# Attention feeding a max-out MLP on one core: the PE order and the evacuations laid out anew, the loads kept

## The chip, the core and the metric

The kernel runs on one core of one Trainium2 chip. The core has a matrix engine (TensorE, "PE" in the profile, with its weight loads as "PEld"), a vector engine (VectorE, DVE), an activation engine (ScalarE, ACT), a general engine (GpSimd, POOL), and a queue engine that issues transfers (SyncE, SP). Each engine works through its own instructions in their order and waits on semaphores for the others. The metric is the time of one execution on the device in microseconds (us); the median of several runs is given, with the lowest and the highest.

## The reference

Inputs are q, k and v of shape 8 x 8 x 1152 x 64 (batch, heads, sequence, width) and three weight matrices, all float32. Neighbouring rows of q are averaged, attention is computed with the 576 pooled queries against 1152 keys, and the result, 4608 tokens of 512 features, goes through a small MLP that takes the larger of two products.

```python
q_pool = q.reshape(B, H, S // 2, 2, D).mean(axis=3)
scores = np.matmul(q_pool, k.transpose(0, 1, 3, 2)) / np.sqrt(D)
attn = softmax(scores)                       # over the keys
x = np.matmul(attn, v)                       # -> (B * S/2, H * D)
out = np.maximum(x @ w1, x @ w2) @ w_out
```

## The kernel before, in words

Two heads are handled together as a pair; there are 32 pairs (4 for each batch entry). The MLP is rewritten: max(x w1, x w2) w_out = relu(x (w1 − w2)) w_out + x (w2 w_out). So there is one hidden product with `wd` = w1 − w2, and the output product adds a term with `w21` = w2 w_out.

The work consists of these kinds:

- **Loads** of q, k, v and weights, issued by SP (lines 343 to 383). Each waits until its raw buffer is free.
- **Casts** on POOL: keys (L405), pooled queries (L435), values (L445), and copies of the last 64 query columns of a pair's exponentials (L468, the "rest").
- **Transposes**: keys by a transfer on SP (`ktrans`, L475); queries by eight 32-row block transposes a pair on VectorE (`qtrans_dve`, L485), from pair 5 on. The first pairs use PE instead.
- **Score groups** (`scores`, L302): 324 groups of 512 columns for two heads. Each is made of 64-row matmuls that run in couples, one for each half of the array, and fills two PSUM banks. A pair has 10 and a bit of them.
- **Exponentials** (`exps`, L317) on ScalarE, one for each group, from the two banks to SBUF.
- **Value products** (`av_jobs`): a "chunk" is nine 128-row matmuls into one bank (L621); a pair has eight. A leftover of 64 query rows is 18 narrower matmuls (L636). VectorE divides by the row sums (L651, L654) and so empties the bank. Two jobs a pair; the last pair of each batch entry also takes the leftovers of the entry's four pairs.
- **Transposes of x** by transfers on SP or by PE, to `xT`.
- **Hidden products** (`h_jobs`, L760): eight couples of 64-row matmuls into two banks, up to 512 columns wide; then relu, on VectorE (L771) or ScalarE (L775).
- **Output products** (`p_job`, L803): 24 couples for 256 tokens into two banks, copied out by VectorE (L809) or ScalarE (L812), stored by SP. The last two blocks are made by `z_job` (L846).

In hidden and output jobs the second half of the couples uses the other row halves. Its first unit has a "fence": it waits on PE's own semaphore until the job's earlier matmuls have completed.

All banks come from eight PSUM banks. A job or a score group may write its banks only after the evacuation of what was there before.

**What sets the order.** Nothing is planned when the program is built: the order is written out as a string of 2712 letters near the end of the kernel (L959 to L987), one letter for one operation: `S` a score group, `E` an exponential, `A` one unit of a value job, `a` one evacuation of it, digits `0` to `3` a unit of an open MLP job (up to four open at once), `4` to `7` its evacuation on VectorE, `8`, `9`, `+`, `-` the same on ScalarE, `r` a query transpose on VectorE, `k`, `q`, `v`, `e` casts on POOL, `l` a load, `t` and `x` transposing transfers, `o` a store. `BANKS` names the bank that each score group or job takes, `MOE` the order of hidden and output jobs, `LOADS` the order of the loads. The function `step` (L925) turns each letter into an operation; the class `Plan` (L17) finds the semaphore waits from what each operation reads and writes. An engine's order is the order of its letters in the string; the place of a letter among those of other engines means nothing beyond the data it needs, with one exception. A load of q, k or v also waits for an exponential ("pace"), and which one depends on where the load stands in the string:

```python
def pace():
    g = done[0] - PACE          # done[0]: the last exponential in the string so far
    return [f"E{g}"] if PACE and g >= PACE_FROM else []
```

Of the kernel before, what the change touches and what calls it, by code (L numbers as in the profile page):

```python
# [116 lines left out]
def bass_funnel_attn__then__act_maxout2_kernel(  # L117
# [11 lines left out]
    E = moe_w_out.shape[1]  # L129
# [33 lines left out]
    FILLS = 16  # L163
    PACE = 2
    PACE_FROM = 40
    FOUR = 1
# [15 lines left out]
    )  # L182
    MOE = (
        "wwhhhhpphhhhpphhhhhhhhpphhhhpphhhhphhhhpphhhhphhhhphhhhpphhhhhhhhhphphh"
    )
    BANKS = (
        "0124605424023623462032424660232342630240624702402064202420472042646264246024604640164604264126402406"
        "0240260240246304260346204040640606062061262062062402740264062402406402640642704260202402402406401640"
        "6460462056204620462046042164206204620620426026402602602602604604614646046046024604604204620420642040"
        "6406406742064264264206520640260462620620162062046206240620206204230642042042424126426046046045620642"  # L190
        "6024062046206206206206412640246056046206404024024026423236042642042626260262626426454526420642064206"
        "2454"
    )

    ctx = ExitStack()
    with ctx:
# [131 lines left out]

        def pace():
            g = done[0] - PACE  # L330
            return [f"E{g}"] if PACE and g >= PACE_FROM else []

        done = [0]
        issued = [0]
# [8 lines left out]
        def load_k(i, lo=0, hi=NT, eng="SP"):  # L343
            b, h0, s = i // NHP, 2 * (i % NHP), i % 3
            old, name = behind() if eng == "SP" else ([], [])
            op(eng, lambda e: e.dma_start(  # L346
                kraw[s][:, :, lo:hi, :].rearrange("p h t d -> p h (t d)"),
                k[b, h0:h0 + 2, :, :].rearrange("h (p t) d -> p h (t d)", t=NT)[
                    :, :, lo * D:hi * D]),
                after=([f"kraw0.{c}" for c in K0] if s == 0 and hi - lo == NT else []) + pace() + old,  # L350
                w=([f"kraw0.{lo}"] if hi - lo < NT else [f"kraw{s}"]) + name,
                dma=f"d_kp{lo}" if hi - lo < NT else f"d_k{s}",
                cost=0.2 * (hi - lo) + 0.03 if hi - lo < NT else 1.45 + 0.6 * (i == 1), tag=("L", "k", i))

        def load_q(i, lo=0, hi=QU, eng="SP"):
# [6 lines left out]
                w=([f"qraw0.{lo}"] if hi - lo < QU else [f"qraw{s}"]) + name,  # L362
                after=(["qraw0.0", "qraw0.4"] if s == 0 and hi - lo == QU else []) + pace() + old,
                dma=f"d_qp{lo}" if hi - lo < QU else f"d_q{s}",
# [10 lines left out]
        def w_load(part, c):  # L375
# [5 lines left out]
                src.rearrange("(c p) f -> p c f", p=P)[:, c * n:(c + 1) * n, :]),  # L381
                w=[f"{key}{c}"] + name, after=old, dma=f"d_w{part}{c}", cost=1.34, tag=("L", "w", part, c))

# [541 lines left out]
        def step(c):  # L925
# [5 lines left out]
            elif c == "E":  # L931
                g, go = exp_at.pop(0)
                go()
                done[0] = g
            elif c in lines or c in "0123":
# [23 lines left out]
        for c in (  # L959
            "luFFlulllfyKQklgfbSkKEFlgFKSgESyFFlKEFgQSbESlFkSFEFFKlEySFSgESlqFFEFQlSbEFkSQElbKvSEgSlESceAAEATcESA"  # L960
            "EAhlkSaSEaASclEKAEglSAEcSAElvSaTaEhElTcSAESlAhAEScAElSSAcEAAlAqESa0a00aE0la0ScAE0SldQEaa00bSd0lEXSj0"
            "00ESvTl0h0E00eS4SlEAAkAEAlSa1ad1E1S1SEl1q1S1E1Kl1g1qE1S1SE1lQkrAEbArSdtAErArSE11avlEa1S5AElSdArESSrA"
            "dArEArSAEkAlaAaSEaAdatAESaXadjXEjSjSEXq0jl00jE0S0qr0E0lSr01rE11e41Sl1E1Sk1r10Er005St0ESv00r0ESSr0rvE"
            "lA4AAEASqalSaEAArAErAlSrSEEaAeaAArxAErSSaAEaAklrAAErS1at1ak1E1r0Sr0xE0r0Sr11E1rS1r0E050Sl0E0q0SrS0tE"
            "r01r10Er0eS0r0E0r0Skr0lE0r1S0r0E0rlSv0r1E14S11El1S1oSE1oAAEASAkEAaAlaSAEtAvSa1aE1SxS11ES111E1111ES11"
            "l1ESq5AAEAlSrSoEAroArAESrkSArEAaAalAEAaAaSvaaEtaSSrXEqArAjAEAjSrle00Ea0aS0rSE0lr0vSr0E1r01rlE114S11E"
            "1S1rSEA5AlvAEASr0E0ta0Eva0SrSE00xe00SE4AAkAESSlAEAaAaAEAlSa1aE1Sx000E0Sk11E0lS11E11S50qlE00tS00ESer0"
            "0rSE00rS0rE00r00Er0l0qSrSE0r01l1r0E14S11E1l1SroSE1r1o11roSErAoArAtEkArAAaaAArq1ESaa1E1Sx001r001E1r0S"
            "1rE0l001rS141E1rS1r1ES5AAEvAAroSSrvoESAlAAEvAaAaAlEAaAkaSa000SaEt0a000011114Ee111S111115E1S111Xl5EvS"
            "j00j0ESl0qSE0000SEl4AAAEArSSaEAaArAlqEArS1a1taE11rSESrE1e1xrS1r1EA5AAEASla0kaE0Sr00rSEq0l0r0SEr0ArAl"  # L970
            "E4SAAESr11aE1a1Srx1ESr11r1SEt5qAAAEArSe0aE0a0Slr0SEkr0S0r0E0lrS0r0E0r0Sl0rE0000ES0S0Er0tArAEArArS0aE"
            "0aq0Srx10Er1S14k1E1S11EroS1rSo1E1oAAoEvAAS1vElSAAlEAvAaSa1ESalAaAAEASa1aE1taS1rXvE1rS1j11Ej1eSrl11rE"
            "11qrSS5EAlAAkEAroS0a0oEa0S0rS0ErAAlAEASa0a0E0l0S4x00E0qSE0r00E0trSA4eAEAArS1a1Ea1k1Sr11ESr1lSr1E5AAA"
            "lEArS1a1Ea11Srx00E10S1l1E1S500tE0Sq0rS0Er00r0e0ESr00rSEl0kr00r0E0rS0l0ES00SE0A4AAEAAaAoaAoASaoSqaE11"
            "x11SESkr11t1rE11rE11rE1SrS1E1r11r1SEr11S1E1S11E1A5AEvAASoSvESlAAoAEvAaAaAElAaAa0Sa0a0E0taS00r0000E04"
            "e0Sx000r0E11141vS1x1E11r100500Sr11qE1Sr01lr110E1rS050E0Sl0r0E0SS0l0E0S0r0EArAArEAArlAkaAaArSE0etEa0a"
            "S0r0SE0rxS0rq0EA4AAEASkao1aE11o1SSE11lS11EA5AAElASa1aE1Sx0r00E0rS1rt0E0er0Sr0E1S4111ESl1r0q0E500S0lE"
            "0SrS0r0EA4lAAEAAAaaAASa1aESlk1Sx1r1ES1r11Ert11r11Er1qSSr1E1rArAEvAS1E11klS11El11vS1E1S1lvA5ESAAEAoAa"
            "oSaSESaAtaArAEArq00Ea0aSa00rExSv0r00ErS0xe0r0E0rSSr0kl0E0S00E0Sl00E0S00El0A4AEAAAaoSaSEoArAtArE00Ea0"
            "0aeS00rxE1111r00qS411E1111151S1k1E1r1Sl00500ESr000SrEl0A4AAEArSla1aE1S1S1EAAAEAlSa1aE1tSrS1rq1E1r1x1"  # L980
            "1rESSre11Er11rSk1Elr11S1E11Sl1E1A5AAEASaoSaEAoAAoEAoSa0a0tEq00rSESr0E00rx00k040E0AArvAArSrSvElArArAE"
            "AvaAaAAaAaSaSaE00a001x14E11S11E1x11Sv511E100S1SE0r1t11r0ES0500E0eSr00Er00SrSE0r00r0SEr0S00E0S00E0004"
            "0E00S0E0oS00oSE4AAAEAAaAaAeAAaEAaAAxAaAaAASa0aES0x00SE1000E0S411E1S11E111500S0E00S11E1S11E1S10E50S00"
            "E0S10E0Se10E00S00E0S00E0S00E10S41E11S11EoS11o1E1oSSo1E1AAEAAAaAaAAAaAaAxAAAAAaAaAAaAa1a1a1a11X1j11j1"
            "11111900001111111150000111o080110091o110000008101110191101000018111009101110000080101111191100000001"
            "001111910000000011111111110001000800110000o008001o11o00010181111Z9ZZZZZoZZoZZZZZZmZZZZzzZZZZZZZZZZmZ"
            "ZZZZZZzZzmzz"  # L987
        ):
            step(c)
# [52 lines left out]
```

## Time and profile before

| What | us |
|---|---|
| Runs (3), median | 358.55 |
| lowest, highest | 357.37, 358.76 |
| Profiled execution, first to last instruction (span) | 356.4 |
| PE busy | 346.0 (97%) |
| ScalarE busy | 313.8 (88%) |
| VectorE busy | 230.1 (65%) |
| POOL busy | 151.4 (42%) |
| Exponentials (L317, 336 instructions), busy | 302.4 |
| Output products (L803, 816 matmuls), busy | 76.4 + 40.8 |
| Value products (L621, 2304 matmuls), busy | 60.7 + 19.7 |
| Query transposes on VectorE (L485, 216), busy | 101.4 |
| POOL idle ahead of the pooled query cast (L435) | 61.1 |

"Busy" is the time in which at least one instruction of the group was running. Of the profiled execution only the span is given, so what lies around it is seen only by holding the span against the runs. Matmuls overlap: one of 512 columns is shown as 0.38 us long, though the next couple starts 0.22 us later. A gap of PE shorter than that difference is not seen as idle time. The chain of waits, which goes back from the last instruction, shows the pace better. "issue" is a time in which an engine waited for nothing that the profile shows.

### The profile page before, as it was taken

The page shows a single profiled execution, that of the slowest core. Times are in us where ns is not written, and L with a number is a line of the kernel's source. Part 1 is how long each engine was busy: PE and PEld are TensorE (multiplying, and loading weights), DVE is VectorE, ACT ScalarE, POOL GpSimd, SP SyncE. Part 2 cuts the span into 40 slices and gives each one's busy share as a digit, 9 for nine tenths or more (in the row PEclk, how much of TensorE's full clock was granted, in tenths as well). Part 3 has the DMA queues.
Part 4 walks back from the last instruction along what each step waited for, and adds up shares of the span by engine and source line. Part 5 has one row for each costly group of instructions (what it writes and reads, how often), then busy time and mean ns, then how long its engine had stood idle before and what let it go on. Part 6 is the DMA issues. An engine that isn't in the chain of part 4 may idle for free.

```text
span 356.4 us, 13757 instructions
## 1 busy us (share of the span) xinstructions
PE 346.0 (97%) x6178; PEld 218.5 (61%) x6178; DVE 230.1 (65%) x472; ACT 313.8 (88%) x354; POOL 151.4 (42%) x136
## 2 busy tenths in 40 slices
PE   7889999999899999999999999999999999999996
PEld 5556665656564675656666576556576757448753
DVE  2587589974966867985887677785586875414001
ACT  5999999999999899999999989989999796992431
POOL 2625997554564264355544455227444621010000
PEclk9999999999999999999999999999999999999999
DMA  8999999999989989998999699998999943012215
GB/s 271 403 397 398 370 255 309 280 289 261 293 252 279 315 196 350 237 301 183 278 320 260 153 230 301 237 314 234 224 299 255 267 68 75 17 32 47 61 31 148
DMA packets 76699, 84.55 MB, mean 237 GB/s; under 512 B 48480, under 2 KB 49760, under 8 KB 76640
## 3 DMA queue, kind: packets, MB, share of 16 engines
q1 hardware_dynamic: 75856, 83.15, 87.5%
q8 instruction: 48, 0.79, 0.9%
q10 hardware_dynamic: 784, 0.52, 0.5%
q14 instruction: 11, 0.09, 0.1%
HBM read 62.91 MB, written 9.44 MB: 203 GB/s over the span
## 4 chain that ended last, share of the span: by engine, by line
PE 87%; ACT 9%; DMA 2%; issue 1%; SPq 0%; DVE 0%
PE ps L803 25%; PE ps L621 20%; PE ps L302 19%; PE ps L760 16%; ACT et L317 9%; PE ps L636 3%; PE ps L593 2%; DMA qraw<-in_q_dram 2%; PE ps L846 1%; PE ps L552 0%; PE ps L533 0%; SPq L346 0%; DVE qp L428 0%; SPq L358 0%; PE ps L730 0%
## 5 line engine op out<-in xcount | busy, mean ns | idle before, releaser
L317 ACT ACTIVATE et<-ps 128x1024 bf16<-128x1024 f32 (+1 forms) x336 | 302.4, 1019 | 14.5 <-PE ps L302 9.7
L302 PE MATMUL ps<-qpT,kT 64*128 64x256 bf16 (+7 forms) x1162 | 117.3, 283 | 2.7 <-issue 1.1
L485 DVE STREAM_TRANSPOSE qpT<-qp 32x288 bf16<-32x288 bf16 x216 | 101.4, 469 | 10.4 <-PE ps L302 6.1
L760 PE MATMUL ps<-xT,wd 64*128 64x512 bf16 (+3 forms) x832 | 81.2, 311 | 0.2
L302 PEld LDWEIGHTS ps<-qpT,kT 64*128 64x128 bf16 x1162 | 48.3, 94 | 49.7 <-ACT et L317 11.3
L803 PE MATMUL ps<-wo,stage 64*128 64x512 bf16 x544 | 76.4, 376 | 0.0
L435 POOL TENSOR_TENSOR qp<-qraw 128x576 bf16<-128x576 f32 x30 | 42.1, 1406 | 61.1 <-DMA qraw<-in_q_dram 57.3
L621 PEld LDWEIGHTS ps<-vE,et 128*128 128x128 bf16 x1728 | 54.9, 97 | 13.9 <-ACT et L317 9.3
L621 PE MATMUL ps<-vE,et 128*128 128x65 bf16 x1728 | 60.7, 193 | 0.7 <-issue 0.3
L771 DVE TENSOR_SCALAR stage<-ps 128x1024 bf16<-128x1024 f32 (+3 forms) x41 | 39.7, 970 | 21.1 <-PE ps L760 20.6
L760 PEld LDWEIGHTS ps<-xT,wd 64*128 64x128 bf16 x832 | 35.6, 94 | 22.2 <-PE ps L760 1.9
L405 POOL TENSOR_SCALAR kbf<-kraw 128x1152 bf16<-128x1152 f32 x31 | 35.7, 1153 | 26.3 <-DMA kraw<-in_k_dram 25.6
L803 PE MATMUL ps<-w,xT 64*128 64x512 bf16 x272 | 40.8, 377 | 0.0
L803 PEld LDWEIGHTS ps<-wo,stage 64*128 64x128 bf16 x544 | 26.4, 94 | 20.5
L445 POOL TENSOR_SCALAR vE<-vraw 128x1152 bf16<-128x1152 f32 x24 | 27.4, 1154 | 19.4 <-PE ps L636 10.8
L809 DVE COPY stage<-ps 128x1024 f32<-128x1024 f32 x14 | 17.1, 1224 | 23.1 <-PE ps L803 23.0
L468 POOL TENSOR_SCALAR stage<-et 128x1152 bf16<-128x1152 bf16 x14 | 16.1, 1152 | 35.5 <-ACT et L317 35.5
L654 DVE TENSOR_TENSOR xnat<-ps,rc 128x256 bf16<-128x256 f32 (+2 forms) x71 | 27.6, 397 | 2.0
L651 DVE RECIPROCAL rc<-ps 128x4 f32<-128x4 f32 (+2 forms) x64 | 11.6, 182 | 25.9 <-PE ps L621 25.5
L621 PEld LDWEIGHTS ps<-stage,et 128*128 128x128 bf16 x576 | 18.1, 97 | 2.7 <-issue 2.6
L621 PE MATMUL ps<-stage,et 128*128 128x65 bf16 x576 | 19.7, 193 | 0.0
L803 PEld LDWEIGHTS ps<-w,xT 64*128 64x128 bf16 x272 | 12.5, 94 | 8.8 <-DVE stage L771 0.2
(55 smaller groups left out, 155.4 us busy)
## 6 DMA issues: line engine op xcount, KB each, us to landing
vraw<-in_v_dram SPq DMA_DIRECT2D x32, 576.0 KB, 6.1
kraw<-in_k_dram SPq DMA_DIRECT2D x31, 576.0 KB, 6.7
qraw<-in_q_dram SPq DMA_DIRECT2D x31, 576.0 KB, 6.3
out_dram<-stage SPq DMA_DIRECT2D x24, 256.0 KB, 4.1
out_dram<-stage SPq DMA_DIRECT2D x21, 128.0 KB, 3.4
xT<-in_moe_w_dram SPq DMA_DIRECT2D x4, 512.0 KB, 12.2
stage<-in_moe_w_out_dram SPq DMA_DIRECT2D x4, 512.0 KB, 14.1
stage<-in_moe_w_dram SPq DMA_DIRECT2D x4, 512.0 KB, 13.2
```

The costliest lines, as they stand in the source:

```text
L302: last = e.matmul(ps[:, h, col:col + hi - lo], kT[i % 3][rows(h), t, :], qpT[i % 3][rows(h), lo:hi], start=True, stop=True)
L317: op("ACT", lambda e: e.activation(et2[:, :, c:c + z - a], ps[:, :, a - g * W:z - g * W], EXP, scale=scale), r=[f"b{m}", f"b{m + 1}"], w=w ...
L405: op("POOL", lambda g: g.tensor_scalar(kbf[s][:, :, :, :].rearrange("p t h d -> p h t d"), kraw[r][:, :, :, :], 1.0, 1.0, ALU.mult, ALU.mu ...
L435: op("POOL", lambda g: g.tensor_tensor(qpf[s][:, :, :], qraw[r][:, :, 0, :], qraw[r][:, :, 1, :], ALU.add), r=[f"qraw{r}"], w=[f"qp{s}.0", ...
L445: return g.tensor_scalar(vE[r][:, :, :, 0:D].rearrange("p t h d -> p h t d"), vraw[s][:, :, :, :], 1.0, 1.0, ALU.mult, ALU.mult)
L485: op("DVE", lambda e: e.transpose(view[dst:dst + 32, :, 32 * pb:32 * pb + 32], qpf[s][src:src + 32, :, 32 * db:32 * db + 32]), r=[f"qp{s}. ...
L621: last = e.matmul(fb[m][:, at * 66:at * 66 + 65], et[:, a:a + P], vE[vs][:, t, half, 0:65], start=(t == 0), stop=(t == NT - 1))
L654: todo.append(evac_op("DVE", lambda e, m, z=z, at=at, num=num, dst=dst: e.tensor_tensor(dst, a(m)[z, at:at + num, 0:D], rc[k][z, at:at + n ...
L760: last = e.matmul(fb[m + k][:, 0:size], wd[z, ct, (f0 + k) * P:(f0 + k + 1) * P], xT[z, ct, n0:n1], start=(turn == 0 and ct == 0), stop=(t ...
L771: return e.tensor_scalar_max(gT[:, f0:f0 + 2, g0:g0 + size], wide[m // 2][:, :, 0:size], 0.0)
L803: last = e.matmul(fb[m + k][:, :], lhs, rhs, start=(turn == 0 and j == 0), stop=(turn == 1 and j == NC_ + NF - 1))
L809: return e.tensor_copy(osb2[:, o:o + 2, :], wide[m // 2][:, :, :])
```

## The change

The diff replaces data: the string of letters, `BANKS` and `MOE`. The letters of PE, ScalarE and VectorE come in another order, and their share of value products that lie behind the scores is different. `MOE` exchanges the places of some output and hidden jobs. At the end, up to four MLP jobs are open at once where two were before (digits `2` and `3`). Loads, stores, casts and their order are kept: since a load's place among the exponentials in the string is no longer the same, the number of the exponential that it waits for is now read from a list, one entry for each load of SP, −1 for none.

```diff
-    PACE = 2
-    PACE_FROM = 40
...
+    PACES = (
...
+        -1, -1, -1, -1, -1, -1, -1, -1, 40, 43, 47, 49, 50, 55, 56, 58, 61, 66, 70, 72, 74, 77, 82, 84,
...
+        270, 275, 276, 284,
+    )
     MOE = (
-        "wwhhhhpphhhhpphhhhhhhhpphhhhpphhhhphhhhpphhhhphhhhphhhhpphhhhhhhhhphphh"
+        "wwhhhhpphhhhpphhhhhhhhpphhhhphhphhphhhhpphhhhphhhhhphhhpphhhhhhphhhphhh"
     )
     BANKS = (
-        "0124605424023623462032424660232342630240624702402064202420472042646264246024604640164604264126402406"
...
+        "2043621402461601603423662504672627074620642702402064202420472042646264246024604640164604264126402406"
...
-        def pace():
-            g = done[0] - PACE
-            return [f"E{g}"] if PACE and g >= PACE_FROM else []
-
-        done = [0]
+        def pace(eng="SP"):
+            g = PACES[issued[0] - 1] if eng == "SP" else -1
+            return [f"E{g}"] if g >= 0 else []
+
...
         for c in (
-            "luFFlulllfyKQklgfbSkKEFlgFKSgESyFFlKEFgQSbESlFkSFEFFKlEySFSgESlqFFEFQlSbEFkSQElbKvSEgSlESceAAEATcESA"
...
-            "11111900001111111150000111o080110091o110000008101110191101000018111009101110000080101111191100000001"
-            "001111910000000011111111110001000800110000o008001o11o00010181111Z9ZZZZZoZZoZZZZZZmZZZZzzZZZZZZZZZZmZ"
+            "lululllllylflFFflKQgklbkSKFElFgKSlgSEFFKFElygQSbSElkFSFEFFKlySEgEFlqSSEFFFQSlEbkFSQEKblvgSESElcSeEAl"
...
+            "2213332211112023330+090011311272211011135023432222330006o0130o111321-1112050100011001223011110922220"
+            "+0000001232311000218333113o30000o330o02003431133533333223333232-Z6ZZZZoZZZoZZZZZZmZZZZzzZZZZZZZZZZmZ"
             "ZZZZZZzZmzz"
         ):
             step(c)
```

The load functions call `pace(eng)`, and the loads of weights call `pace()` too, with entries of −1. The line that set `done[0]` in `step` goes.

66 lines of the change are left out of this document (33 added, 33 removed), and 4 rows, old and new, of the table PACES.

## The prediction

> **What bounds the kernel now.** I read the page first, then the stretches of the span (the windows view), then the chain of waits stretch by stretch, then who waits for whom.
>
> ```profile
> span 356.4 us, 13757 instructions
> PE 346.0 (97%) x6178; PEld 218.5 (61%) x6178; DVE 230.1 (65%) x472; ACT 313.8 (88%) x354; POOL 151.4 (42%) x136
> PE 87%; ACT 9%; DMA 2%; issue 1%; SPq 0%; DVE 0%
> ...
> core 0: us, PE busy (x) PEld busy (x) DVE busy (x) ACT busy (x) POOL busy (x), PEclk, DMA share, GB/s
> 0.00:52.00 52.00, 46.46 (x942) 30.24 (x944) 33.15 (x64) 47.11 (x54) 31.15 (x37) 1.00 1.00 356
> 52.00:100.00 48.00, 46.58 (x800) 28.18 (x797) 37.90 (x80) 47.39 (x53) 26.82 (x23) 1.00 1.08 284
> 100.00:320.00 220.00, 219.72 (x3872) 137.21 (x3870) 153.72 (x314) 207.99 (x233) 93.46 (x78) 1.00 0.92 226
> 320.00:356.40 36.40, 33.23 (x576) 22.86 (x572) 5.30 (x16) 11.34 (x18) 0.00 (x0) 0.99 0.30 74
> ```
>
> PE is the bound: 87% of the chain that ended last is PE, at full clock. What matters more for this change is where PE stands idle. Before 52 us it lacks 5.54 us (52.00 − 46.46), from 52 to 100 us 1.42, from 100 to 320 us only 0.28. The last 3.2 us of the last stretch are the final copy and store, after the last matmul. A new order can remove only idle time and whatever extra PE time the order itself causes; the matmuls stay.
>
> The profiled execution has a span of 356.4 us; the runs took 357.37, 358.55 and 358.76, so the median stands 2.15 us above it (358.55 − 356.4). I make the sum against the span and add 2.15.
>
> **What the change leaves alone.** Counted in the two step strings of the diff, every kind of operation occurs equally often, except that four evacuations of the last two products go from ScalarE to VectorE (14 to 10). The orders of POOL and of the SP queue are the same from first to last. PE's order is the same for its first 155 units, up to score group 49, which starts at about 52 us; before that only bank numbers are exchanged. So the 5.54 us of the start are not touched, and I cost the exchanged banks at nothing: the units before and behind each other are the same, and the first loads set that stretch. The loads still wait for exponentials, now from a list; worked through the old string, the old formula gives the same number for each of the 78 loads that wait (40 for the first, 284 for the last). The SP queue therefore issues at the same exponentials as before, with the same queue ahead of each load, and no wait is added there. The PE work left behind the last exponential is 31.8 us before and 32.1 after, so the end is no shorter.
>
> **Term 1: changes of tile shape.** PE runs 64-row products (scores, hidden, output) and 128-row ones (value products).
>
> ```profile
> 61.39 0.54 PE ps L302 x8
> ...
> 63.67 1.19 PE ps L621 x36
> ...
> 66.93 0.86 PE ps L760 x8
> ...
> 119.43 2.28 PE ps L621 x72
> ```
>
> Here the columns are start, length, engine, tile, line and count of a piece of the chain. Eight hidden matmuls are four pairs in 0.86: 0.215 a pair of 512 columns. Two runs of 36 value matmuls take 2 × 1.19 = 2.38, one run of 72 takes 2.28: a change of shape costs 0.10. Likewise two score groups take 0.54 where four pairs would be near 0.43. In the strings I count 172 changes of shape before and 168 after. More value runs stand between scores (from value product to score 53 to 57 times, from score to value product 39 to 45), but fewer lie next to hidden and output products. Four fewer at 0.10: **−0.4 us**. All of it is on PE and so on the path.
>
> **Term 2: halves of a hidden product that stand back to back.** Each hidden job has eight units; the fifth swaps the row halves and waits for PE's own earlier matmul to complete (the fence in its part).
>
> ```profile
> 131.52 0.45 PEld L760 LDWEIGHTS ps<-xT,wd 64*128 64x128 bf16 x16 [0.24 <-PE ps L760]
> 132.21 0.17 PEld L760 LDWEIGHTS ps<-xT,wd 64*128 64x128 bf16 x6 [0.24 <-PE ps L760]
> 133.12 0.10 PEld L760 LDWEIGHTS ps<-xT,wd 64*128 64x128 bf16 x2 [0.24 <-PE ps L760]
> ```
>
> Three times the fifth unit directly follows the fourth of its own job, each time PE stands 0.24. In the new string something stands between in all but one case, a job of 256 columns. Two fewer at 0.24: **−0.5 us**. Other fences have at least one unit between them in both orders, and a 0.216 unit covers nearly all of it.
>
> **Term 3: the one long stall.**
>
> ```profile
> 91.57 1.12 issue
> 92.70 0.61 PE ps L302 x8
> ...
> q8 instruction: 48, 0.79, 0.9%
> q8 instruction: 1, 0.02, 1.4%
> ```
>
> Between score groups 91 and 92 PE waits 1.12 us for nothing that the profile shows. In the stretch from 88 to 93 us (the last row, from the DMA view of that stretch) one of the 48 instruction blocks arrives. The stall sits at the end of a dense run of value matmuls, which use up instructions fastest. If it is a fetch that came late, it is an accident of where the blocks fall, and a new order moves it. It may go (−1.1) or stay or recur elsewhere (0). I take half: **−0.5 us**, between ends of −1.1 and +1.1 (a second one). [...]
>
> **Term 4: waits for ScalarE, which come as well as go.**
>
> ```profile
> L317 ACT ACTIVATE et<-ps 128x1024 bf16<-128x1024 f32 x312 | 291.3, 1049 | 11.5 <-PE ps L302 9.7 <-PE ps L552 0.9
> L812 ACT COPY stage<-ps 128x1024 f32<-128x1024 f32 x3 | 3.0, 1012 | 12.1 <-PE ps L803 12.1
> PEld ps L302 <- ACT et L317: 9.4, 42, 0.4
> PEld ps L621 <- ACT et L317: 8.8, 25, 0.6
> ...
> 60.13 1.26 PE L621 MATMUL ps<-vE,et 128*128 128x65 bf16 x36 [0.25 <-ACT et L317]
> ...
> 150.67 1.26 PE L621 MATMUL ps<-vE,et 128*128 128x65 bf16 x36
> ```
>
> A full exponential takes 0.93 us of ScalarE (291.3 / 312). These waits of the weight loads (from 52 us on) lie mostly under the matmul before them: PE's own idle in the same time is 1.70, 1.12 of it the issue stall. So scores already arrive just when a bank comes free, and the only larger wait is 0.25 at 60.13. The new order starts value products nearer to the last score of their pair: within 1.5 us of PE work for pairs 7, 8, 9, 13, 20, 26, 27 and 31, where the old one, past the start, has only 8 and 14. Pairs 7, 27 and 31 begin with the leftovers of three other pairs ahead of their own, and are safe. The others stand at 1.39 us, just as pair 14 does in the old order; that pair began at 150.67 with no gap in PE. The list also moves three evacuations of the last products into the time of exponentials, at most 1.01 each, against 12.0 us that ScalarE stands idle from 100 to 320 us. I take +0.1 at each of four new tight places and −0.2 for 60.13, where the bank that pair 4 takes was filled by a score 1.8 us of PE work earlier instead of 1.4: **+0.2 us**, between −0.25 (that wait gone, none new) and +2.0 (0.25 at each of eight).
>
> **Term 5: VectorE.** Its in-order queue holds the 216 transposes of q, of which the last of a pair must be done before that pair's first score.
>
> ```profile
> 67.31 2.90 DVE L485 STREAM_TRANSPOSE qpT<-qp 32x288 bf16<-32x288 bf16 x6
> 70.22 1.23 DVE L771 TENSOR_SCALAR stage<-ps 128x1024 bf16<-128x1024 f32 x1
> ```
>
> The new order places them later. For pair 7 the last stands 0.9 us of PE work ahead of its first score (4.1 before), for pairs 10 and 15 at 1.9; the least before was 1.7, at pair 6. One transpose is 0.48 (2.90 / 6), so pair 7 still makes it if VectorE is at most one transpose behind; behind an evacuation of 1.23 it is up to 0.8 late (1.23 + 0.48 − 0.9). I take 0, with 0.8 as the bad end and 0 as the good one. The four evacuations that VectorE takes over lie where it is busy 5.30 of 36.40 us: nothing.
>
> **The sum.** −0.4 − 0.5 − 0.5 + 0.2 + 0 = −1.2: a span of 355.2 and a time of **357.3 us**, 0.3% less (355.2 + 2.15, rounded down).
>
> **The rivals.** *All the avoidable idle goes.* 1.42 + 0.28 from 52 us on, 0.4 for shapes, and the fences, of whose 0.7 PE's own rows show little, since a matmul still draining counts as busy: −2.8, 355.7 us. For it: the new order reaches all of the stretch in which this idle lies. Against: ScalarE's waits are not removed by order as long as it is 95% busy (207.99 of 220). *Nothing is gained.* New waits eat the 0.9 us of terms 1 and 2 and the stall recurs: 358.6 to 360.4 us (the bad ends of terms 4 and 5, 2.0 + 0.8, less 0.9). For it: tight places such as 0.64 us between the last value product of pair 12 and the score that takes its bank, which VectorE must empty in between, and the 0.9 of pair 7's transposes. *Value casts come too late*, the case on the other side:
>
> ```profile
> 56.78 1.16 POOL L445 TENSOR_SCALAR vE<-vraw 128x1152 bf16<-128x1152 f32 x1
> 75.33 1.15 POOL L445 TENSOR_SCALAR vE<-vraw 128x1152 bf16<-128x1152 f32 x1
> ...
> 78.76 0.99 PE L621 MATMUL ps<-vE,et 128*128 128x65 bf16 x27
> ...
> POOL vE L445 <- DMA vraw<-in_v_dram: 7.8, 5, 2.9
> ```
>
> The loads keep their exponentials while value products move up to them. Pair 4's cast ends at 57.9 and its product started at 60.13; by the string it comes about 1.2 earlier (2.35 nearer to its last score, which itself stands 1.5 later, and without the 0.25 wait), at 58.9. Pair 6's cast ends at 76.5 and its product, at 78.76 before, comes 1.3 earlier (1.73 less 0.43), at 77.5. Both then have 1.0 us to spare. A load that is late by 2.9, the longest wait of these casts, would cost 1.9 at each: +3.8, 361.1 us. It decides from a delay of 1.0 us on, and makes the kernel slower by over 0.5% from 2.5 at both. Against it: POOL, SP and the exponentials that release the loads are unchanged, so the casts should end where they do. That the change does nothing at all is ruled out, since PE's order differs from unit 155 on.
>
> **How the numbers follow.** The forecast gets 0.57, everything gone 0.16, nothing gained 0.17, late casts 0.10. About 0.5% (1.8 us) is what a measurement can tell from no change here: faster means below 356.8, slower above 360.3. Of the forecast's own range, 356.0 to 358.6, some three tenths lie below 356.8: 0.17, and with the second case 0.33. Slower: 0.10 and the worst of "nothing gained" (0.04): 0.14. The rest, 0.53, is no change. The range runs from 354.9 to 360.4. Its lower end is everything gone (355.7) less two thirds of the 1.18 by which the lowest run lies under the median; its upper end is the worst of "nothing gained". It leaves out the late casts and little else.
>
> **What would show it.** PE's idle from 100 to 320 us stays under 1 us; the 0.24 waits of hidden products on themselves fall from three to one in the 128-column job; no issue stall of 1 us near 91 us; PE's matmul count stays 6178 and its last matmul ends about 1 us earlier. Wrong would be: idle of PE ahead of L621 ended by POOL (late casts), ahead of L302 ended by VectorE's transposes near pair 7, or ScalarE's last exponential ending over 1 us later.

## The result, and the profile after

The changed kernel takes **372.74 us** (median of 6 runs, 369.06 to 378.24) against 358.50 us for the kernel before (6 runs beside them, 357.37 to 358.76). The ratio is 1.0365, with a 95% interval of 1.0324 to 1.0406: slower by 3.6%, some 13 us, where 357.3 us was forecast and 360.4 us was the upper end of the range. Two of the six runs, 374.94 and 378.24 us (granted clock 0.991 and 0.973), lie over 1.5% above the fastest; here and below such runs count in a median and not in a ratio. The profiled execution of the changed kernel took 369.06 us. It is the fastest of its six, so the traces show 10.9 us of the loss (a span of 367.3 against 356.4 us).

Lines of the code stand five or six further down than before: scores are now L308, exponentials L323, value products L626, hidden products L765, output products L808, and VectorE's copy of an output block is L814. First the head of the page, with the engines and the chain that ended last:

```profile
span 367.3 us, 13741 instructions
PE 349.7 (95%) x6178; PEld 219.8 (60%) x6178; DVE 233.1 (63%) x476; ACT 311.3 (85%) x350; POOL 151.0 (41%) x136
PE 69%; ACT 18%; DMA 7%; issue 2%; DVE 2%; POOL 1%; SPq 1%; POOLq 0%
```

The 6178 matmuls are all there. PE's share of the chain fell from 87% to 69%, and transfers and ScalarE have taken its place. The stretches of before, with one difference: the last one ends at 356.4 us, 10.9 us ahead of this kernel's end.

```profile
0.00:52.00 52.00, 47.33 (x938) 30.89 (x938) 32.74 (x63) 46.79 (x54) 30.69 (x36) 1.00 0.98 353
52.00:100.00 48.00, 47.94 (x814) 28.80 (x810) 36.50 (x77) 47.26 (x53) 25.84 (x23) 1.00 1.05 256
100.00:320.00 220.00, 210.25 (x3742) 132.94 (x3742) 151.13 (x314) 199.75 (x225) 93.36 (x78) 0.99 0.90 230
```

From 52 to 100 us PE stands idle 0.06 us, against 1.42 before: the issue stall at 91.57 us is gone. From 100 to 320 us it stands idle 9.75 us (220.00 − 210.25), against 0.28. Nearly all of that is four stalls. Who waited for whom (the columns are the total, the number of times, and the longest):

```profile
POOL qp L440 <- DVE qpT L490: 34.8, 8, 7.7
ACT et L323 <- PE ps L308: 20.8, 20, 2.7
...
PEld ps L765 <- DMA xT<-xnat: 4.9, 2, 2.5
PE ps L765 <- DMA xT<-xnat: 4.1, 2, 2.1
PE ps L308 <- DVE stage L814: 2.7, 1, 2.7
```

Scores wait once for VectorE's copy of an output block, and hidden products wait for transposed x. Between the start of one matmul and the next the four gaps are 3.10 us (to 118.80), 2.35 (to 226.24), 2.77 (to 263.41) and 2.33 (to 300.89). Less the usual 0.2 us each (a couple of 512 columns takes 0.215), that is 9.75 us. ScalarE's new idle time ahead of exponentials follows from these: PE gives it no scores.

**The first stall** is in VectorE's queue. First the chain of waits, with start, length and what ran; then VectorE's own instructions there.

```profile
106.53 6.10 DMA qraw<-in_q_dram
...
112.70 1.41 POOL qp L440
...
117.52 1.24 DVE stage L814
118.75 0.05 issue
118.80 0.76 PE ps L308 x6
119.56 0.85 PE ps L808 x4
120.41 2.10 PE ps L626 x36
```

```profile
114.14 3.37 DVE L490 STREAM_TRANSPOSE qpT<-qp 32x288 bf16<-32x288 bf16 x7 [4.71 <-POOL qp L440]
117.52 1.23 DVE L814 COPY stage<-ps 128x1024 f32<-128x1024 f32 x1
```

The new order puts the copy of output block 2 behind seven query transposes of pair 12. These wait 4.71 us for POOL's cast, which waits for the load of q. The last matmul of the block ends at 114.57 us, while the transposes run until 117.51. So the copy of a finished block waits 2.9 us for them, and score group 117, which needs the block's banks, stands on PE.

**The other three** come out of SP's queue. This is SP in the kernel before and in the changed one, around output block 7:

```profile
199.03 1.31 SPq L475 DMA_TRANSPOSE kT<-kbf  x1
204.70 0.65 SPq L829 DMA_DIRECT2D out_dram<-stage  x1
205.44 0.54 SPq L370 DMA_DIRECT2D vraw<-in_v_dram  x1
...
209.54 1.35 SPq L703 DMA_TRANSPOSE xT<-xnat  x1
```

```profile
202.09 1.31 SPq L480 DMA_TRANSPOSE kT<-kbf  x1
214.46 0.65 SPq L834 DMA_DIRECT2D out_dram<-stage  x1
215.15 0.76 SPq L375 DMA_DIRECT2D vraw<-in_v_dram  x1
...
219.22 1.34 SPq L708 DMA_TRANSPOSE xT<-xnat  x1
```

The order of the transfers is the same. Behind the key transpose SP stood 4.4 us before (200.34 to 204.70), and stands 11.1 us now (203.40 to 214.46), at the store of block 7. In the strings the copy of block 7 moved from ahead of exponential 208 to behind 213. The transfer of x of pair 19, whose data had been there since 212.60, starts at 219.22 instead of 209.54, lands 6.97 us after its start, and hidden job 6 goes on at 226.24.

Job 7 waits for x of pair 23 and job 9 for x of pair 27, and there the queue is not all of it. Ahead of job 7 no store holds SP for long. A load of values that waits for POOL's cast holds it until 251.75, and then a key transpose, that of pair 27:

```profile
254.55 4.58 SPq L480 DMA_TRANSPOSE kT<-kbf  x1
259.18 1.28 SPq L708 DMA_TRANSPOSE xT<-xnat  x1
```

The x behind it had been ready since 254.99, so it starts 4.2 us late; in the kernel before, it was ready at 250.23 and started at 250.84. Ahead of job 9 SP stands 3.2 us at a store of block 11 (2.9 before), and x of pair 27 starts only 1.25 us after its data. But it takes 5.31 us to land, where it took 3.70 in the kernel before. Why it took longer is not shown.

One cost more goes with a stall. In windows of 1 us the clock (the third number from the end) falls behind the first one:

```profile
119.00:120.00 1.00, 1.00 (x10) 0.28 (x6) 0.96 (x3) 0.77 (x1) 0.00 (x0) 0.57 0.97 359
120.00:121.00 1.00, 1.00 (x15) 0.66 (x14) 0.23 (x1) 1.00 (x2) 0.17 (x1) 0.50 1.11 436
121.00:122.00 1.00, 1.00 (x23) 1.00 (x21) 0.00 (x0) 0.17 (x1) 0.98 (x1) 0.50 0.93 369
122.00:123.00 1.00, 1.00 (x18) 0.64 (x15) 0.42 (x2) 0.09 (x1) 0.67 (x1) 0.73 1.10 406
```

It lost 0.43 + 0.50 + 0.50 + 0.27 = 1.70 us of full speed, and 36 value matmuls took 2.10 us there instead of 1.19. So 9.75 and 1.70 make 11.45 us, and 1.36 us were gained from 52 to 100 us. That leaves 10.1 of the 10.9 us by which the span grew. By this estimate some 0.8 us more lie where the profile shows no idle time.

The ratio rests on three more runs, 2.0 to 5.1 us longer in span than the profiled one. Their mean granted clock was 0.985 to 0.991 against 0.995. One minus the clock, times the span, gives an estimate of what that cost: 3.7 of the 5.1 us, and about 1.5 us in each of the other two. No trace of them was kept.

### The profile page after: what moved, and what is told of

Read it like the earlier page. It is cut to its first block, busy times and chain, and to the rows that moved or that the text cites. A ratio compares the mean times of both kernels' runs of the same rounds, so it can differ in the third digit from the quotient of the medians.

```text
span 367.3 us, 13741 instructions
## 1 busy us (share of the span) xinstructions
PE 349.7 (95%) x6178; PEld 219.8 (60%) x6178; DVE 233.1 (63%) x476; ACT 311.3 (85%) x350; POOL 151.0 (41%) x136
## 4 chain that ended last, share of the span: by engine, by line
PE 69%; ACT 18%; DMA 7%; issue 2%; DVE 2%; POOL 1%; SPq 1%; POOLq 0%
PE ps L808 19%; ACT et L323 18%; PE ps L626 16%; PE ps L308 15%; PE ps L765 11%; DMA qraw<-in_q_dram 4%; DMA xT<-xnat 3%; PE ps L641 2%; PE ps L598 2%; PE ps L851 1%; PE ps L520 1%; DVE qpT L490 1%; POOL qp L440 1%; PE ps L557 1%; SPq L480 1%
## 5 line engine op out<-in xcount | busy, mean ns | idle before, releaser
L323 ACT ACTIVATE et<-ps 128x1024 bf16<-128x1024 f32 (+1 forms) x336 | 302.7, 1024 | 23.3 <-PE ps L308 20.8
L308 PE MATMUL ps<-qpT,kT 64*128 64x256 bf16 (+7 forms) x1162 | 118.2, 285 | 4.2 <-DVE stage L814 2.7
L490 DVE STREAM_TRANSPOSE qpT<-qp 32x288 bf16<-32x288 bf16 x216 | 101.4, 469 | 10.1 <-POOL qp L440 6.3
L765 PE MATMUL ps<-xT,wd 64*128 64x512 bf16 (+3 forms) x832 | 84.4, 311 | 6.6 <-DMA xT<-xnat 4.1
L308 PEld LDWEIGHTS ps<-qpT,kT 64*128 64x128 bf16 x1162 | 47.9, 94 | 51.7 <-ACT et L323 14.5
L808 PE MATMUL ps<-wo,stage 64*128 64x512 bf16 x544 | 77.9, 378 | 0.0
L776 DVE TENSOR_SCALAR stage<-ps 128x1024 bf16<-128x1024 f32 (+3 forms) x45 | 42.1, 939 | 45.0 <-PE ps L765 44.5
L626 PEld LDWEIGHTS ps<-vE,et 128*128 128x128 bf16 x1728 | 55.7, 98 | 14.0 <-ACT et L323 10.0
L626 PE MATMUL ps<-vE,et 128*128 128x65 bf16 x1728 | 61.5, 194 | 0.6 <-ACT et L323 0.5
L765 PEld LDWEIGHTS ps<-xT,wd 64*128 64x128 bf16 x832 | 36.5, 94 | 31.2 <-DMA xT<-xnat 4.9
L808 PE MATMUL ps<-w,xT 64*128 64x512 bf16 x272 | 40.7, 377 | 0.0
L808 PEld LDWEIGHTS ps<-wo,stage 64*128 64x128 bf16 x544 | 26.5, 94 | 19.4 <-issue 0.2
L814 DVE COPY stage<-ps 128x1024 f32<-128x1024 f32 x14 | 17.1, 1224 | 11.3 <-PE ps L808 11.1
L626 PEld LDWEIGHTS ps<-stage,et 128*128 128x128 bf16 x576 | 18.1, 97 | 3.1 <-issue 3.1
L626 PE MATMUL ps<-stage,et 128*128 128x65 bf16 x576 | 19.7, 193 | 0.3 <-issue 0.3
L808 PEld LDWEIGHTS ps<-w,xT 64*128 64x128 bf16 x272 | 12.5, 94 | 8.3 <-PE ps L808 0.3
```

Source lines behind the costliest of these rows:

```text
L308: last = e.matmul(ps[:, h, col:col + hi - lo], kT[i % 3][rows(h), t, :], qpT[i % 3][rows(h), lo:hi], start=True, stop=True)
L323: op("ACT", lambda e: e.activation(et2[:, :, c:c + z - a], ps[:, :, a - g * W:z - g * W], EXP, scale=scale), r=[f"b{m}", f"b{m + 1}"], w=w ...
L490: op("DVE", lambda e: e.transpose(view[dst:dst + 32, :, 32 * pb:32 * pb + 32], qpf[s][src:src + 32, :, 32 * db:32 * db + 32]), r=[f"qp{s}. ...
L626: last = e.matmul(fb[m][:, at * 66:at * 66 + 65], et[:, a:a + P], vE[vs][:, t, half, 0:65], start=(t == 0), stop=(t == NT - 1))
L765: last = e.matmul(fb[m + k][:, 0:size], wd[z, ct, (f0 + k) * P:(f0 + k + 1) * P], xT[z, ct, n0:n1], start=(turn == 0 and ct == 0), stop=(t ...
L776: return e.tensor_scalar_max(gT[:, f0:f0 + 2, g0:g0 + size], wide[m // 2][:, :, 0:size], 0.0)
```

## The experiments

**Theory Q** says that the loss comes from two in-order queues. On SP, stores wait for copies that now come later, and the x transfers and loads behind them wait too. On VectorE, a copy stands behind transposes whose data is late. **The rival L** says that the loads keep exponentials that no longer suit the work: they start too late for the new order, and the chain through the q load at 106.53 us is that. Each ratio below is to the kernel before on the same chip, with its 95% interval. The headings number the kernels as the expectations do.

### Kernel 1: stores of the output blocks later on SP

```diff
 SP around output block 7 (O = store, kt = key transpose, xt = x transfer)
-    kt 22, O7, load v 23, O7, load q 24, kt 23, xt 19, xt 19
+    kt 22, O6, O6, O6, load v 23, load q 24, kt 23, xt 19, xt 19
     (O7 just ahead of the copy of block 8; so for blocks 1 to 13)
```

> The changed kernel; on the SP queue alone each output block's stores (blocks 1 to 13) stand just ahead of the next block's evacuation instead of just behind their own. Theory Q (the queue orders were kept although the evacuations that they wait for have moved; SP stands at a store whose block is not ready, and the transposing transfers of x behind it come late): the three PE waits ahead of hidden products (2.14 us at 224, 2.58 at 261, 2.28 at 298) fall below 0.3 us each, the profiled span goes from 367.3 to about 360.5, the time from 372.7 to about 366. Theory L (the loads are released too late for the new order, whatever stands ahead of them): the SP idle time ahead of stores goes but the loads still wait for their exponentials, and PE's waits stay within 1 us in sum; 371 to 373 us. Theory W (PE's new order itself meets ScalarE's exponentials badly): no change.

Measured: 363.25 us (4 runs), ratio 1.0114 (1.0069 to 1.0159). The waits of hidden jobs 6 and 9 are gone; that of job 7 is 1.5 us, where less than 0.3 was expected. So moving stores alone takes back 2.5 of the 3.65%: most of the loss came through the order on SP.

### Kernel 2: the copy of block 2 ahead of the transposes on VectorE

```diff
 VectorE
-    7 query transposes of pair 12, copy of block 2
+    copy of block 2, 7 query transposes of pair 12
```

> The changed kernel; on VectorE alone the evacuation of output block 2 stands ahead of the seven query transposes of pair 12 that stood ahead of it. Theory Q: the 2.89 us PE wait at 116 us goes, and with it the two stretches at half TensorE clock behind it (about 1.5 us more): span about 363, time about 368. Theory L: the score group of pair 12 then waits for the same late load of q instead; at most 1 us of gain. Theory W: no change.

Measured: 370.25 us (4 runs), ratio 1.0337 (1.0302 to 1.0372). The stall at 116 us is gone from the trace and the three of the hidden jobs stay (2.6, 2.8 and 2.2 us). In the times this is worth 0.3%, where some 368 us, 1.2%, was expected, and the interval overlaps with that of the changed kernel. The trace shows one reason: the clock now falls behind two of the other stalls (225.3 to 228.8 and 262.9 to 266.4 us, 1.7 us lost each), behind which it had stayed up, and the profiled span is 368.7 us against 367.3. So the place is shown, its price is not.

### Kernel 3: both

The two edits together, on the changed kernel.

> The changed kernel with both edits, the late stores and the evacuation ahead of the transposes. Theory Q: the sum of both, 7 + 4.4 us: span about 356, time 358 to 361, no more than 0.7% above the kernel before. Theory L: 369 us or more. Theory W: no change.

Measured: 361.59 us (10 runs), ratio 1.0083 (1.0051 to 1.0116). 2.8 of the 3.65% are taken back by moving the stores of thirteen blocks and one copy, with PE's order untouched. The interval overlaps with that of kernel 1, so the copy's share is not priced here either. One long wait is left, ahead of hidden job 7, at 256.62 us. SP's queue in this kernel shows why: the key transpose of pair 27 holds the queue until 251.31, and the x transfer of pair 23 behind it, whose data was there at 249.64, starts 1.7 us late.

```profile
249.16 2.15 SPq L480 DMA_TRANSPOSE kT<-kbf  x1
251.35 2.39 SPq L708 DMA_TRANSPOSE xT<-xnat  x1
```

### Kernel 4, rival L: every load four exponentials earlier

```diff
-    PACES = ( ... 40, 43, 47, 49, ... 270, 275, 276, 284 )
+    PACES = ( ... 36, 39, 43, 45, ... 266, 271, 272, 280 )
```

> The changed kernel with every load released by an exponential four earlier (about 3.8 us), nothing else moved. Theory Q: loads behind a blocked store still stand behind it, so the three waits ahead of hidden products stay (sum above 5 us); only the wait at 116 us may go; 367 to 373 us. Theory L: the late loads come 3.8 us earlier and at least 6 of the 10 us of new PE waits go; 362 to 366 us. Theory W: no change.

Measured: 373.33 us (4 runs), ratio 1.0389 (1.0315 to 1.0463). No gain: rival L falls, as far as four exponentials test it. The loads cannot use the earlier exponentials, since SP reaches them no sooner. The load of q at 106.53 us now starts at 106.00, behind a key transpose (100.89 to 104.49) and an x transfer (until 105.95), and at the store of block 7 SP still stands 10.5 us (201.77 to 212.23).

### Kernels 5 and 8: the x transfers first

Kernel 5 is kernel 3, and each x transfer goes right behind the copies that it reads, past the loads, key transposes and stores between, and the key transpose of pair 27 goes behind the x transfers of pair 23.

```diff
 SP, one of the places
-    load q 17, load k 17, kt 16, xt 12
+    xt 12, load q 17, load k 17, kt 16
```

> The kernel of e3_both, with the transposing transfers of x placed on the SP queue right behind the evacuations that they read, ahead of loads, key transposes and stores that stood before them (and ahead of the key transpose of pair 27 for pair 23). Theory Q: the last long PE wait for such a transfer in e3_both, 1.5 us at 255 us, goes; span 357.9 to about 356.5, time about 360, within 0.5% of the kernel before. If PE's new order has a cost of its own (Theory W), the time stays at 361.5 with the wait gone and others in its place.

Measured: 363.01 us (6 runs), ratio 1.0133 (1.0107 to 1.0160): worse than without, where better was expected. PE in this kernel:

```profile
225.94 0.39 PE L308 MATMUL ps<-qpT,kT 64*128 64x320 bf16 x4 [1.23 <-DVE stage L776]
...
251.63 0.43 PE L626 MATMUL ps<-stage,et 128*128 128x65 bf16 x9 [1.72 <-issue]
...
260.56 0.61 PE L765 MATMUL ps<-xT,wd 64*128 64x256 bf16 x8 [1.60 <-issue]
```

Score group 230 now waits for VectorE, and job 7 is still late. The row between is of another kind: a value chunk that waits on no semaphore stood 1.72 us (see kernels 11 and 12), and it makes the x of its own pair, 23, for which job 7 then waits. The x transfer then starts 0.03 us after its data, but takes 7.3 us to land, against 3.9 in the changed kernel. So the edit does not test the queue cleanly. What it shows is that x ahead of all else is no better order.

In kernel 8, the 21 query transposes that stood ahead of copies of finished products on VectorE were put behind them as well. (The 46 of the expectation are the pairs of a transpose and a copy that change their order.)

> The kernel of e5_x_first, with VectorE's evacuations of output, hidden and value jobs moved ahead of the query transposes that stood between a job's last matmul and its evacuation (46 transposes change places). Theory Q: banks come free sooner and no evacuation stands behind a transpose whose data is late; up to 1 us less than e5_x_first and less spread between runs; 358.5 to 360 us. If transposes were then late for their scores, slower by up to 1 us.

Measured: 362.74 us (6 runs), ratio 1.0119 (1.0086 to 1.0153), no different from the one above. The wait of score group 230 stayed (1.58 us between starts). Of the places tried, block 2 is the only one where VectorE's order cost a stall that an exchange removes.

### Kernels 6 and 7: such steps done to the kernel before

If the queue is the cause, the old order must suffer too when its SP is spoilt. First the late stores alone, on the kernel before.

> The kernel before, with the same late stores as in e1_stores_late. In its trace SP also stands at stores, up to 13.8 us, but PE waits for no transfer of x. Theory Q: SP's idle time only matters where PE waits behind it, so no change, within 0.3% of the kernel before. If late stores were good by themselves (fewer transfers at the same time), 1 us or more less.

Measured: 359.71 us (12 runs), ratio 1.0044 (1.0017 to 1.0071). The edit that gained 2.5% on the changed kernel costs 0.4% here: late stores are no virtue of their own, they mend a queue whose copies come late.

Then the x transfers of pair 19 were put four loads and a key transpose further back, around the first store of block 8:

```diff
 SP of the kernel before
-    kt 23, xt 19, xt 19, load k 24, load v 24, load q 25, load k 25, kt 24, xt 20, O8
+    kt 23, load k 24, load v 24, load q 25, load k 25, kt 24, xt 19, O8, xt 19, xt 20
```

> The kernel before, its order of PE, ScalarE and VectorE untouched; on SP the two transposing transfers of x of pair 19 stand behind the first store of output block 8 instead of ahead of the loads before it. That store is issued at 223.5 us, and hidden block 6 begins at 223.6. Theory Q: the transfers then land some 5 us later than PE needs them, PE waits 4 to 6 us ahead of hidden block 6 and its clock falls for a while; time 5 to 8 us above the kernel before. Theory W (the new PE order is to blame, not the queue): under 1 us.

Measured: 360.44 us (10 runs), ratio 1.0066 (1.0038 to 1.0095). The chain there:

```profile
213.43 4.70 ACT et L317 x5
218.13 0.02 issue
218.15 0.37 SPq L346
...
220.32 6.96 DMA xT<-xnat
227.28 0.05 issue
227.33 0.39 PE ps L760 x2
```

The first of the two transfers starts at 220.32 instead of 209.54, 10.8 us later. It also takes 6.96 us to land instead of 5.39, so it lands 12.3 us later (at 227.28 instead of 214.93). Hidden job 6 stands 2.13 us, as in the changed kernel (9.7 us later, 2.0 us). So one late x transfer makes such a stall in the old order as well. The loss was smaller than expected: what holds the queue is a load of keys that waits for an exponential, and between that transfer and its reader lay some 10.2 us of slack (12.3 − 2.1).

### Kernels 9 and 10: one key transpose, and fewer stores

Kernel 9 is kernel 3 with the key transpose of pair 27 behind the x transfers of pair 23, nothing else:

```diff
 SP
-    kt 27, xt 23, xt 23
+    xt 23, xt 23, kt 27
```

> The third kernel (late stores of blocks 1 to 13, evacuation of output block 2 ahead of the transposes of pair 12) with one more exchange on SP: the key transpose of pair 27 goes behind the two x transfers of pair 23. Theory Q (the order on SP): the wait of 1.55 us at 255 us ahead of hidden job 7 falls by the 2.1 us for which the key transpose held the queue, so it goes wholly; pair 27's scores stand too far behind to be late. Span about 356.4 to 356.8 against 357.9, time about 1.3 us under the third kernel's: 360.2, ratio to the kernel before 1.002 to 1.007. Rival (each exchange on SP makes another transfer late, as in the fifth kernel): the wait at 255 goes and one of 1 us or more comes at another x transfer or key transpose behind it; ratio 1.007 to 1.013.

Measured: 360.23 us (12 runs, 357.94 to 363.52), ratio 1.0042 (1.0013 to 1.0070). The time is the one that was expected of theory Q. But the interval overlaps with that of kernel 3, and the profiled span, 359.0 us, is above kernel 3's 357.9, where 356.4 to 356.8 was expected. What the trace shows for theory Q is that job 7's wait is gone, with no wait of over 1 us for transposed x in its place. The stretch from 100 to 320 us:

```profile
100.00:320.00 220.00, 218.27 (x3870) 136.72 (x3870) 154.57 (x319) 209.10 (x235) 93.41 (x78) 1.00 0.92 230
```

PE's idle time there is 1.73 us, against 9.75 in the changed kernel. Of this 1.16 is one stall inside a value product, below. With three exchanges in two queues, 3.2 of the 3.65% are taken back.

In kernel 10 only the stores of blocks 1, 7, 10 and 11 are late.

> The ninth kernel, but only the stores of output blocks 1, 7, 10 and 11 are moved back (the ones ahead of which SP waited longest before x transfers that PE needed); those of the nine other blocks stay where the changed kernel has them. Theory Q: the loss of the changed kernel came from these few places, so this is within 0.5% of the ninth kernel, with no wait of PE over 1 us for xT. Rival (the stores wait too long everywhere and the whole queue drifts late): waits for xT over 1 us come back at hidden jobs 7 or 9, and the time is 2 us or more above the ninth kernel's.

Measured: 361.93 us (8 runs), ratio 1.0082 (1.0051 to 1.0112). The wait of job 7 is back (2.12 us between starts), those of jobs 6 and 9 are not. The rival has the wait, theory Q the size (1.7 us above kernel 9; within 0.5% was 1.8): undecided between them, but the other stores ahead of pair 23 matter too. Here it is not the order on SP: the x transfer of pair 23 starts 0.03 us after its data, at 251.13, and takes 7.9 us to land against 5.5 in kernel 9, with stores of block 9 just ahead of it (249.27). That these stores slow it is not shown.

### Kernels 11 and 12: is the stall of 1.12 us the instructions?

In several traces PE stood for no reason that the profile shows in the middle of a value chunk, nine matmuls that wait on nothing but ahead of the first. This is kernel 9, and the DMA view from 133 to 134 us of it:

```profile
133.84 0.87 PE L626 MATMUL ps<-vE,et 128*128 128x65 bf16 x23
135.87 0.30 PE L626 MATMUL ps<-vE,et 128*128 128x65 bf16 x4 [1.16 <-issue]
```

```profile
q8 instruction: 1, 0.02, 6.7%
```

A block of instructions arrives from 133.56 to 134.63, and the next matmul starts 1.24 us later. The same is seen in kernel 1 (block until 134.37, 2.30 us of stall, next matmul at 135.63), and in the kernel before the block ends at 91.40 and score group 92 starts at 92.70. To test it, PE's stream of instructions was shifted in the kernel before, by the length of the first warm-up product:

```diff
-    FILL = 28
+    FILL = 44        (and 12 in a second kernel)
```

> The kernel before with one number changed: the first warm-up product of the matrix engine, which runs from 1.12 us while nothing else is ready (its next work starts at 4.08), has 44 matmuls in place of 28. Nothing else changes; the 16 more take about 0.9 us in that gap and delay nothing. They push every later instruction of the engine 16 matmuls further from the start of its stream. Theory F (the stall at 92 us is a block of instructions that comes late, tied to the place in the stream): the stall of 1.1 to 1.5 us comes 16 matmuls earlier in the order of the work: no longer ahead of score group 92, but inside the run of 54 value matmuls, after about 42 of them, in the middle of a chunk. Rival (tied to score group 92 and what it needs): it stays ahead of that group with its length. Time within 0.3% of the kernel before in both.

> The same with 12 matmuls in place of 28, 16 fewer. Theory F: the stall comes 16 matmuls later than before: score groups 92 and 93 (4 each) run on without it, and it falls among the twelve transposing matmuls behind them, after about eight; it may be shorter there, since these and the scores are longer per instruction than value matmuls. Rival: it stays ahead of score group 92. Time within 0.3% of the kernel before in both.

```profile
90.16 1.44 PE L621 MATMUL ps<-stage,et 128*128 128x65 bf16 x42
92.18 0.52 PE L621 MATMUL ps<-stage,et 128*128 128x65 bf16 x12 [0.58 <-issue]
92.63 0.83 PE L302 MATMUL ps<-qpT,kT 64*128 64x64 bf16 x12
```

```profile
93.16 0.87 PE L302 MATMUL ps<-qpT,kT 64*128 64x64 bf16 x12
94.36 0.29 PE L552 MATMUL ps<-ident,xnat 64*128 64x64 bf16 x8 [0.33 <-DVE xnat L654]
94.83 0.27 PE L730 MATMUL ps<-ident,xend 64*128 64x64 bf16 x4 [0.17 <-issue]
```

With 44 the run of 54 value matmuls stops after 42, and score group 92 follows at once. With 12 the stall stands behind eight of the twelve transposing matmuls. Both are the very places that theory F named: the stall belongs to a place in the stream, with a block's end 1.43 and 1.49 us ahead of the next matmul, and not to score group 92. Its length is 0.58 and 0.17 us instead of 1.12. The reason that the expectation has for a shorter stall there holds for scores only. In the kernel before, from start to start, eight score matmuls take 0.43 us (0.054 each) and 54 value matmuls 1.74 (0.032 each), but the twelve transposing ones 0.33 (0.028 each).

The times were 359.30 us (7 runs), ratio 1.0027 (1.0000 to 1.0054), and 360.30 us (3 runs), 1.0098 (1.0028 to 1.0167). The expectation of time was wrong for 12: neither edit was free. The warm-up matmuls take 0.106 us each ((4.08 − 1.12) / 28), later ones about 0.055 (in the kernel before a row of six at 10.36 us is 0.51 long and a row of two at 9.81 us is 0.29), so 44 fill more than the gap; and with only 12, PE is slow for longer (from 8 to 12 us it is busy 4.00 us with 45 matmuls, before 3.24 us with 62). Score group 80 starts 0.71 us later with 44 and 1.98 later with 12. Of the 1.98, some 0.8 come with another stall that moved: with 12, PE stands 1.12 us at 31.49 inside a value product, 1.31 us behind a block's end, where the kernel before stands 0.35 us at 29.04, sixteen matmuls earlier. These delays are older than the stall, and they allow the best reading of what it is worth: group 94 starts 0.69 and 1.58 us later. Half the stall gone gave 0.02 us, nearly all of it 0.40. With 44 the value products behind it now wait 0.16 us for ScalarE instead.

None of these kernels beats the kernel before.

## Why the prediction was wrong

**The step that failed** is in the part on what the change leaves alone: "The SP queue therefore issues at the same exponentials as before, with the same queue ahead of each load, and no wait is added there." The order on SP was the same, and so were the exponentials of the loads. But stores and x transfers stand in that queue as well, and wait for copies, not for exponentials. Where the new order places a copy later, SP waits at its store, with all behind it: 11.1 us instead of 4.4 at block 7. Three of the four stalls (about 7 of 9.75 us) are waits for x transfers that came late through this queue, and moving the stores alone took back 2.5 of 3.65%. Only for job 6 is the trace as plain as that. Ahead of job 7 it was a key transpose that held the queue, and ahead of job 9 the queue explains 1.25 of 2.1 us, while the transfer itself took 1.6 us longer. For every store and transfer the string showed where its copy had gone. Only the loads were worked through.

**Term 5** named the right engine and looked at one side only. It asked whether the transposes come in time for their own pair's scores, and gave 0.8 us as the bad end, at pair 7. That place did not stall (its last transpose ends at 71.67, its score group 70 starts at 71.96). The loss came from a copy behind the transposes, at pair 12, with 2.7 us and a slower clock behind it (1.7 us). The prediction had looked at a place of this kind: "0.64 us between the last value product of pair 12 and the score that takes its bank, which VectorE must empty in between". That place, score group 137, did not stall. It counted among the tight places for the rival "Nothing is gained", priced at 2.8 us in all, and of none did the prediction ask what VectorE has queued ahead of the copy.

**The rivals.** The one on the slow side, late value casts, was a wrong mechanism: no wait of PE on POOL's values shows in the waits of the changed kernel. It shares its ground with the right one, a transfer that keeps its place while its readers and writers move, but its reason against itself ("POOL, SP and the exponentials that release the loads are unchanged") is the same mistake.

**What held.** Term 2: the halves of a hidden product stand on each other in one place (0.34 us) instead of three (0.24 each). It is a job of 256 columns, as the term says; the list of signs calls it a 128-column job. And the weight loads' waits of that kind fell from 7 (1.9 us) to 5 (1.5 us).

Term 3: the stall at 91.57 us went, as half expected, and the reason given for it, a block that came late, is supported by the shifted streams, with which the stall moved by 16 matmuls; no run shows it directly. But its worth was mis-sized: with 1.1 us as the whole and 0.5 as the middle, where the runs give 0.0 to 0.4, since behind the shifted stall PE waits 0.16 us for ScalarE (kernel 11), and ahead of it 0.33 us for VectorE (kernel 12). And it recurs elsewhere, 1.16 and 0.94 us in kernel 9. The trace of the kernel before has 48 blocks and this one long stall beside them, that of the changed kernel 48 and none. The rival of kernels 11 and 12, that the stall is tied to score group 92, is refuted: it moved away from that group with the stream.

Term 4: ScalarE's banks made no new stall of PE. PE's waits for exponentials are 0.6 us ahead of scores and 0.5 us ahead of value products, over the whole run (0.5 and 0.3 before).

Term 1, four changes of shape for 0.4 us, is below what any run here could tell, and stays open. Nothing of the forecast saving is seen: with the long waits but one taken out, in kernel 3, PE is busy 347.7 us against 346.0 in the kernel before, for the same matmuls at full clock, and idle 10.2 against 10.4. What the new order adds there is in busy time, in waits too short to show or in changes of shape, and no run tells these apart. Open as well is the last 0.42% between kernel 9 and the kernel before. Kernel 9's profile has two stalls without a shown cause in it, 1.16 and 0.94 us, but no run took these away in that kernel.

## What to carry to other kernels

The SP queue kept its order here and not its times: its stand at the store of block 7 grew from 4.4 to 11.1 us. When producers are moved, go through every instruction of every queue that waits for one of them, stores included, and ask what stands behind it. Where the work of one queue is kept and that of the others is laid out anew, an order that was good can become one in which finished data waits behind unfinished data, and here the remedy was to move the entry that waits, not the one that is late (stores on SP, 2.5 of 3.65%). The stall of 1.12 us was worth 0.0 to 0.4 us, with waits of 0.16 and 0.33 us for other engines beside it: look at what is next before counting a stall as a gain.

## What the runs showed of the hardware

PE's clock fell to half behind some stalls, for 3.4 us or for twice that. Behind the 3.10 us gap of the changed kernel 1.70 us were lost at half speed, which is 3.4 us of half clock. In kernel 7, behind 2.51 us, the four windows from 228 to 232 us show 0.60, 0.50, 0.50 and 0.69: 1.71 us lost, 3.4 us again. In kernel 4, behind 2.84 and 3.57 us, 3.41 us were lost each time, which is 6.8 us of half clock. Behind 2.77, 2.35 and 2.33 us in the changed kernel the clock stayed at 1.00, and behind 3.39 us in kernel 4 as well; behind 2.12 us in kernel 10, 2.49 us in kernel 1 and 2.79 us in kernel 2 it fell. So length alone does not decide. What does was not shown.

Near the end of the arrival of a block of instructions PE stopped, in or just behind a run of short matmuls (54 value matmuls in 1.80 us in the kernel before), and went on 1.2 to 1.5 us after the block's end (1.30 in the kernel before, 1.26, 1.50, 1.24, 1.43 and 1.49 in kernels 1, 5, 9, 11 and 12). That the block is the cause is inferred from this and not shown. The place belongs to the stream: 16 matmuls more ahead of it moved the stop 16 matmuls earlier, 16 fewer moved it 16 later. Its length does not: kernels 1, 3, 9 and 10 have the changed kernel's order on PE and stop at the same matmul for 2.30, 0.28, 1.16 and 0.69 us, the changed kernel not at all.
